# Pooled attention with a mixer behind it: the fourth batch's q right behind the third's v, two buffers for v, and the loads of two batches in a row

## The chip, the core and the metric

The kernel runs on one core of a Trainium2 chip. TensorE (PE) does the matmuls and their weight loads (PEld), VectorE (DVE), ScalarE (ACT) and GpSimd (POOL) the rest; SyncE (SP) issues transfers. All loads of inputs are issued by POOL, which casts them from float32 to bfloat16 on the way; SP issues the transposes that run as transfers, and the stores. The time is device microseconds of one execution, and a kernel's number is the median of its runs.

## What is computed

```python
B, H, S, D = 8, 8, 576, 64            # q, k, v float32
k_p = k.reshape(B, H, 72, 8, D).mean(axis=3)
v_p = v.reshape(B, H, 72, 8, D).mean(axis=3)
attn = softmax(scale * q @ k_p^T)     # 576 x 72 for each head
x = (attn @ v_p) -> (B, S, H * D)     # 8 x 576 x 512
h = relu(x^T @ w_tok1) @ w_tok2       # token mix: 576 -> 256 -> 576
u = x + h^T
out = u + relu(u @ w_ch1) @ w_ch2     # channel mix: 512 -> 1536 -> 512
```

## The kernel before

A batch has 576 rows: 512 "main" rows in four groups of 128, and 64 "tail" rows. Tails are joined in pairs of batches so that they fill 128 partitions: `groups = [[0, 7], [1, 2], [3, 4], [5, 6]]`. For the pairs [3, 4] and [5, 6] one tail unit computes the attention of both batches' tails at once. So the tail of batch 3 needs k, q and v of batch 4 as well.

For batch b the steps are: load k, q, v (`load`, L117); average k by matmuls on PE (`pool_k`, L256) into a block-diagonal operand kbd; average v. Batches 0 and 1 average v by matmuls, and from batch 2 on POOL adds the eight rows of each window (`sum_v`, L293), twelve instructions for each batch, in two-head steps, into vpx. Then come the transpose of q (from batch 2 on by SP as a transfer, `qT_dma`, L547, main and tail), scores (`do_S`, L320 and L420), row maxima and subtraction on DVE, exponentials on ACT (`do_E`), the transposes of the probabilities by SP (`do_PT`, L344 and L445, tile pT), the values (`do_AV`, L358 and L459, matmuls at L391), token mix (`do_AT` L482, `do_u` L506, transposes of u by SP at L522, tile uTm), and channel mix (`channel_mix`, L759): L773 makes GT, L788 the output.

The order on every engine is written by hand: within `manual_schedule` the emission order is the order of each engine's queue, and the loop at L853 weaves two streams for each b by their costs. The main stream is the channel mix of batch b (`c_stream`, L820); the side stream is `value_stream` of batch b + 1 (values and token mix) followed by `score_stream` of batch b + 2 (pooling of k, scores, exponentials, transposes). While c(1) runs, the side stream is thus the values of batch 2 and the scores of batch 3; within the scores of batch 3, k of batch 4 is pooled too, since it owns the shared tail (`owned`, L689).

Loads of batch 2 are issued before the loop (k and q) and early in `second_stream` (v, L659), directly ahead of `sum_v(2)`. Later loads stand behind a gate: `load_gated` (L746) lets POOL copy one column of the last pT of the current batch, so that POOL's queue goes on only when that transpose has landed; then it issues the loads of the batch and runs `sum_v`. With b = 2 the gate brings the rest of batch 3 and batch 4 (L749 to L754).

Buffers: `kv_pool` (km, qm) has two of each, `v_pool` (vs) one, `tail_pool` (kt, qt) two, `gt_pool` two for each width of GT (512 for main rows, 128 for a tail). Batch 1's tails are single tiles, and so is w2r, in which w_tok2 is staged before POOL splits it (`split_w_tok2`, L234).

Of the kernel before, what the change touches and what calls it, by code (L numbers as in the profile page):

```python
# [9 lines left out]
BF16 = mybir.dt.bfloat16  # L10
# [5 lines left out]
class Stream:  # L16
# [5 lines left out]
    def add(self, cost, fn):  # L22
        self.items.append((cost, fn))
# [25 lines left out]
def kernel(  # L49
# [18 lines left out]
    B, H, S, D = q.shape  # L68
# [14 lines left out]

    singles = ctx.enter_context(tc.tile_pool(name="singles", bufs=1))
    kv_pool = ctx.enter_context(tc.tile_pool(name="kv", bufs=2))
    v_pool = ctx.enter_context(tc.tile_pool(name="vp", bufs=1))
    sum_pool = ctx.enter_context(tc.tile_pool(name="sums", bufs=1))
    tail_pool = ctx.enter_context(tc.tile_pool(name="tl", bufs=2))
    pt_pool = ctx.enter_context(tc.tile_pool(name="ptp", bufs=6))
# [5 lines left out]
    at_pool = ctx.enter_context(tc.tile_pool(name="atp", bufs=3))  # L95
    ut_pool = ctx.enter_context(tc.tile_pool(name="utail", bufs=2))
    gt_pool = ctx.enter_context(tc.tile_pool(name="gt", bufs=2))
    out_pool = ctx.enter_context(tc.tile_pool(name="outp", bufs=4))
    ps = ctx.enter_context(tc.tile_pool(name="ps", bufs=6, space=bass.MemoryType.PSUM))
    ps_tr = ctx.enter_context(tc.tile_pool(name="ps_tr", bufs=2, space=bass.MemoryType.PSUM))  # L100
# [11 lines left out]
    tail_t[0] = tail_t[B - 1] = [singles.tile([P, H, D], BF16, name=n) for n in ("kt0", "qt0", "vt0")]  # L112
    for t in tail_t[0]:
        nc.vector.memset(t[half[1]], 0.0)
    tail_t[1] = [singles.tile([P, H, D], BF16, name=n) for n in ("kt1", "qt1", "vt1")]

    def load(b, which=(0, 1, 2)):  # L117
        g = group_of[b]
        if (b == 2 or g > 1 and slot_of[b] == 0) and 0 in which:
            tail_t[b] = [tail_pool.tile([P, H, D], BF16, name=n) for n in ("kt", "qt")]  # L120
            if b == 2:
                for t in tail_t[b]:
                    nc.gpsimd.memset(t[half[0]], 0.0)
            else:
                tail_t[groups[g][1]] = tail_t[b]
        main_t.setdefault(b, [None] * 3)
        for i in which:
            src = (k, q, v)[i]
            if i == 2 and b > 1:

                vs = v_pool.tile([P, H, POOL, D], BF16, name="vs")
                nc.gpsimd.dma_start(out=vs[0:SP].rearrange("p h t d -> p h (t d)"),
                                    in_=src[b].rearrange("h (p t) d -> p h (t d)", t=POOL))
                main_t[b][i] = vs
                continue
            mt = (v_pool.tile([P, H, POOL, D], BF16, name="vs")[:, :, 0:NJ, :] if i == 2 else
                  kv_pool.tile([P, H, NJ, D], BF16, name=("km", "qm")[i]))
            main_t[b][i], tt = mt, tail_t[b][i]
            nc.gpsimd.dma_start(out=mt.rearrange("p h j d -> p h (j d)"),
                                in_=src[b, :, 0:MAIN, :].rearrange("h (p j) d -> p h (j d)", j=NJ))  # L140

            for bb in [b] if g < 2 else groups[g] if slot_of[b] == 0 else []:
                nc.gpsimd.dma_start(out=tt[half[slot_of[bb]]], in_=src[bb, :, MAIN:S, :].rearrange("h p d -> p h d"))
# [72 lines left out]

    w1m = singles.tile([P, NJ, DT], BF16)
    w1t = [singles.tile([P, DT], BF16, name=f"w1t{s}") for s in range(2)]
    w2r = singles.tile([P, 2, S], BF16)
    w2m = singles.tile([P, 2, NJ, P], BF16)  # L220
    w2t = [singles.tile([P, 2, P], BF16, name=f"w2t{s}") for s in range(2)]
    wc1 = singles.tile([P, 4, DC], BF16)
# [426 lines left out]
    def second_stream(st):  # L649

        add = adder(st)
        b = 1
        a, c, t = units(b)
        add(KP, pool_k, b)
        add(QT, a.do_qT)
        add(QT, c.do_qT)
        add(SC, a.do_S, 0)
        add(VP, pool_v, b)
        add(0, load, 2, (2,))  # L659
        add(0, sum_v, 2)  # L660
        add(SC, a.do_S, 1)
        add(0, a.do_E, 0)
        add(SC, a.do_S, 2)
        add(0, a.do_E, 1)
        add(SC, c.do_S, 0)
        add(0, a.do_E, 2)
        add(QT, t.do_qT)
        add(SC, c.do_S, 1)
        add(0, c.do_E, 0)
        add(PT, a.do_PT, 0)  # L670
        add(SC, t.do_S)
        add(0, c.do_E, 1)
        add(PT, a.do_PT, 1)
        add(SC, c.do_S, 2)
        add(0, t.do_E)
        add(AV, a.do_AV, 0)
        add(0, c.do_E, 2)
        add(PT, t.do_PT)
        add(AV, a.do_AV, 1)
        add(PT, c.do_PT, 0)  # L680
        add(PT, c.do_PT, 1)
        add(AV, t.do_AV)
        units(2)
        add(0, qT_dma, 2)
        add(AV, c.do_AV, 0)
        add(AV, c.do_AV, 1)
        mix_stream(st, b, owned(2))
# [37 lines left out]
    def value_stream(st, b):  # L725

        add = adder(st)
        a, c, t = parts[b]
        if b == 2:
            add(0, load_gated, b + 2, lambda: c.pT[1][:, 0, 0:1])  # L730
        if b + 1 < B:
            units(b + 1)
            add(0, qT_dma, b + 1)
        if b != 2 and b + 2 < B:
            add(0, load_gated, b + 2, lambda: c.pT[1][:, 0, 0:1])
        add(AV, a.do_AV, 0)
        add(AV, a.do_AV, 1)
        if t:
            add(AV, t.do_AV)
        add(AV, c.do_AV, 0)  # L740
        add(AV, c.do_AV, 1)
        mix_stream(st, b, owned(b + 1)[:1] if b + 1 < B and b != 2 else ())

    gate = singles.tile([P, 1], BF16)

    def load_gated(b, ready):  # L746

        nc.gpsimd.tensor_copy(out=gate, in_=ready())
        if b == 4:  # L749

            load(b - 1, (1, 0, 2))
            load(b, (0, 1))
            sum_v(b - 1)
            load(b, (2,))  # L754
        else:
            load(b, (0, 2, 1) if slot_of[b] else (0, 1, 2))
        sum_v(b)

    def channel_mix(uTs, us, dst, width, early=0):  # L759

        GT = gt_pool.tile([P, NM, width], BF16, name=f"GT{width}")
        per = 512 // width

        def do_GT(m0):
            def f():
                g_ps = ps.tile([P, per, width], FP32, name="pa")
                for i in range(per):  # L770
                    m = m0 + i
                    for kk in range(4):
                        nc.tensor.matmul(out=g_ps[:, i, :], lhsT=wc1[:, kk, m * P:(m + 1) * P], rhs=uTs[:, kk, :],  # L773
                                         start=(kk == 0), stop=(kk == 3))
                nc.scalar.activation(out=GT[:, m0:m0 + per, :], in_=g_ps, func=AF.Relu)  # L775
            return f

        def out_pieces(j, halves=1):
            n, w = NM // 3, DM // halves
            pieces = []  # L780
            for c in range(halves):
                cols, hold = slice(c * w, (c + 1) * w), {}

                def do_out(part, cols=cols, hold=hold):
                    if part == 0:
                        hold["ps"] = ps.tile([P, w], FP32, name="pa")
                    for kk in range(part * n, (part + 1) * n):
                        nc.tensor.matmul(out=hold["ps"], lhsT=GT[:, kk, j * P:(j + 1) * P], rhs=wc2[:, kk, cols],  # L788
                                         start=(kk == 0), stop=(kk == NM - 1 and us is not None))
                    if part == 2:  # L790
                        o_sb = out_pool.tile([P, w], FP32, name="o")
                        if us is None:
                            for kk in range(4):
                                nc.tensor.matmul(out=hold["ps"][:, kk * P:(kk + 1) * P], lhsT=uTs[:, kk, j * P:(j + 1) * P],
                                                 rhs=ident, start=False, stop=(kk == 3))
                            nc.vector.tensor_copy(out=o_sb, in_=hold["ps"])
                        else:
                            nc.vector.tensor_tensor(out=o_sb, in0=hold["ps"], in1=us(j)[:, cols], op=ALU.add)  # L798
                        dst(j, cols, o_sb)

                for part in range(3):
                    pieces.append((864 / halves, lambda part=part, do=do_out: do(part)))
            return pieces

        def do_early(m, hold, k0):
            def f():
                if k0 == 0:
                    hold[m] = ps.tile([P, width], FP32, name="pa")
                for kk in range(k0, k0 + 2):
                    nc.tensor.matmul(out=hold[m], lhsT=wc1[:, kk, m * P:(m + 1) * P], rhs=uTs[:, kk, :],  # L810
                                     start=(kk == 0), stop=(kk == 3))
                if k0 == 2:
                    nc.scalar.activation(out=GT[:, m, :], in_=hold[m], func=AF.Relu)
            return f

        hold = {}
        wide = [(432, do_early(m, hold, k0)) for k0 in (0, 2) for m in range(early)]
        return wide + [(864, do_GT(m0)) for m0 in range(early, NM, per)], out_pieces
# [74 lines left out]
```

## Time and profile before

| | us |
|---|---|
| median of 3 runs | 305.63 |
| the runs | 301.86, 305.63, 309.34 |
| the profiled execution | 307.68 |
| its span, first to last instruction | 306.0 |
| busy PE, DVE, ACT, POOL | 280.0, 161.2, 120.7, 101.4 |
| matmuls of L788, L773 | 105.9, 94.8 |

The mean granted clock of TensorE in it is 0.961 of full. The two lines of the channel mix are the largest groups, and the chain of work that ended last runs over them, over transfers of v and over POOL's sums (columns: start, length, what):

```profile
77.18 16.25 DMA vs<-in_v_dram
...
103.66 10.29 DMA vs<-in_v_dram
114.09 1.14 POOL s L299
```

The chain's shares by engine:

```profile
PE 68%; DMA 17%; POOL 12%; issue 1%; DVE 1%; ACT 0%; POOLq 0%
```

A chain goes back from the last instruction, at each step to what released it, or to the instruction before it on its engine; PE's share is work, and the shares of DMA and POOL are stretches in which the chain ran over a transfer or over a sum. The three channel-mix stretches that matter begin, by the first L773 of a batch in PE's timeline, at 64.95 (batch 1), 107.42 (batch 2) and 153.37 (batch 3).

### The profile page before, as it was taken

Reading aid. Unit: us, or ns where it says so; the run is one execution under the profiler, and the core shown is the slowest. Engines: PE = TensorE matmul, PEld = TensorE weight load, DVE = VectorE, ACT = ScalarE, POOL = GpSimd, SP = SyncE. Lnnn points to the kernel's source line nnn. Section 1 sums busy time; section 2 is a strip of 40 time slices with the busy share of each in tenths; the row PEclk is TensorE's granted clock in tenths of the full one; section 3 lists DMA queues with packets and bytes.
Section 4 is the critical chain, followed back from the end, with each engine's and each line's share of the span. In section 5 each row is a group of like instructions: output and inputs, shape, how many; then the busy total and the mean of one; then the engine's idle time right before and its main releaser. Section 6 shows DMA issues by size and latency. Waiting matters only on the chain.

```text
span 306.0 us, 5659 instructions
## 1 busy us (share of the span) xinstructions
PE 280.0 (92%) x2242; PEld 148.3 (48%) x2242; DVE 161.2 (53%) x368; ACT 120.7 (39%) x221; POOL 101.4 (33%) x147
## 2 busy tenths in 40 slices
PE   6899999999924938799999999999999999999995
PEld 4574555555402513344654545446544444464463
DVE  4783486787522923227763795368546943430012
ACT  8573893155210423130545336405452353025420
POOL 8675500835407609908430382265000000000000
PEclk9999999999985986599999999999999999999999
DMA  7999999787999999793799999996914850152013
GB/s 89 185 204 195 200 199 161 156 155 135 178 170 125 160 146 205 81 167 106 155 193 134 145 201 220 158 173 127 216 26 86 155 138 1 71 133 56 2 69 104
DMA packets 102714, 42.68 MB, mean 139 GB/s; under 512 B 72480, under 2 KB 98080, under 8 KB 102688
## 3 DMA queue, kind: packets, MB, share of 16 engines
q0 software_dynamic: 36688, 17.93, 45.7%
q1 hardware_dynamic: 65856, 24.26, 43.5%
q8 instruction: 17, 0.28, 0.4%
q10 hardware_dynamic: 144, 0.13, 0.1%
q14 instruction: 9, 0.07, 0.1%
HBM read 35.85 MB, written 9.44 MB: 148 GB/s over the span
## 4 chain that ended last, share of the span: by engine, by line
PE 68%; DMA 17%; POOL 12%; issue 1%; DVE 1%; ACT 0%; POOLq 0%
PE pa L788 27%; PE pa L773 26%; DMA vs<-in_v_dram 13%; PE pa L510 3%; PE pa L476 3%; POOL s L299 3%; DMA w2r<-in_moe_w_tok_dram 3%; PE pa L391 2%; PE pa L327 2%; POOL s L300 2%; POOL vpx L301 1%; DMA pT<-prob_m 1%; PE pa L515 1%; PE pa L480 1%; PE pa L268 1%
## 5 line engine op out<-in xcount | busy, mean ns | idle before, releaser
L788 PE MATMUL pa<-wc,GT 128*128 128x512 bf16 (+1 forms) x444 | 105.9, 378 | 0.0
L773 PE MATMUL pa<-uTm,wc 128*128 128x512 bf16 x372 | 94.8, 395 | 0.0
L775 ACT ACTIVATE GT<-pa 128x512 bf16<-128x512 f32 x105 | 62.3, 597 | 76.3 <-PE pa L773 76.1
L773 PEld LDWEIGHTS <-wc 128*128 128x128 bf16 x564 | 46.2, 100 | 38.8 <-issue 5.1
L788 PEld LDWEIGHTS <-GT 128*128 128x128 bf16 x444 | 41.8, 99 | 40.8 <-issue 1.1
L299 POOL TENSOR_TENSOR s<-vs 72x512 f32<-72x512 bf16 x24 | 27.5, 1147 | 69.7 <-DMA vs<-in_v_dram 68.3
L340 ACT ACTIVATE prob_m<-sh 128x432 bf16<-128x432 f32 (+1 forms) x48 | 24.4, 521 | 60.9 <-DVE sh L332 51.1
L798 DVE TENSOR_TENSOR o<-pa,um 128x512 f32<-128x512 f32 (+1 forms) x29 | 19.4, 669 | 26.0 <-PE pa L788 26.0
L330 DVE TENSOR_REDUCE mx<-pa 128x6 f32<-128x432 f32 (+1 forms) x48 | 26.4, 550 | 9.4 <-PE pa L327 9.3
L395 DVE RECIPROCAL den<-pa 128x4 f32<-128x4 f32 (+1 forms) x66 | 11.7, 177 | 34.5 <-PE pa L391 34.3
L332 DVE TENSOR_TENSOR sh<-pa,mx 128x432 f32<-128x432 f32 (+1 forms) x48 | 26.8, 558 | 5.1 <-ACT GT L775 0.5
L396 DVE TENSOR_TENSOR xm<-pa,den 128x256 bf16<-128x256 f32 x56 | 23.8, 425 | 1.9
L512 DVE TENSOR_TENSOR um<-pa,xm 128x512 bf16<-128x512 f32 x28 | 18.8, 687 | 8.3 <-PE pa L510 8.3
L391 PE MATMUL pa<-vpx,pT 72*128 72x65 bf16 (+1 forms) x280 | 15.0, 199 | 7.5 <-DMA pT<-prob_m 4.7
L391 PEld LDWEIGHTS <-pT 72*128 72x128 bf16 (+1 forms) x280 | 13.2, 104 | 16.8 <-issue 5.9
L327 PE MATMUL pa<-kbd,qT 128*128 128x144 bf16 x128 | 15.9, 231 | 5.3 <-DMA qT<-qm 4.9
L327 PEld LDWEIGHTS <-qT 128*128 128x128 bf16 x128 | 10.8, 100 | 14.8 <-DMA qT<-qm 5.8
L300 POOL TENSOR_TENSOR s<-s 72x256 f32<-72x256 f32 x24 | 17.3, 722 | 1.9
L472 DVE TENSOR_SCALAR AT<-pa 128x512 bf16<-128x512 f32 x8 | 5.5, 692 | 21.7 <-PE pa L480 20.2
L510 PE MATMUL pa<-AT,w2m 128*128 128x512 bf16 x56 | 15.8, 379 | 0.0
L476 PE MATMUL pa<-xm,w1m 128*128 128x512 bf16 x56 | 14.5, 379 | 0.3 <-DVE xm L396 0.3
L254 PE MATMUL pa<-idle 128*128 128x288 bf16 (+2 forms) x36 | 9.9, 405 | 2.2 <-DVE pool_t L179 2.2
(126 smaller groups left out, 236.9 us busy)
## 6 DMA issues: line engine op xcount, KB each, us to landing
out_dram<-o SPq DMA_DIRECT2D x31, 256.0 KB, 2.6
km<-in_k_dram POOLq DMA_DIRECT2D x8, 512.0 KB, 8.9
qm<-in_q_dram POOLq DMA_DIRECT2D x7, 512.0 KB, 11.8
vs<-in_v_dram POOLq DMA_DIRECT2D x6, 576.0 KB, 12.2
wc<-in_moe_w_ch_dram POOLq DMA_DIRECT2D x6, 512.0 KB, 12.6
out_dram<-o SPq DMA_DIRECT2D x9, 128.0 KB, 2.3
vs<-in_v_dram POOLq DMA_DIRECT2D x2, 512.0 KB, 10.1
kt<-in_k_dram POOLq DMA_DIRECT2D x8, 64.0 KB, 7.8
```

The source lines that it names most:

```text
L299: nc.gpsimd.tensor_tensor(out=s4, in0=vs[:, hs, 0:4], in1=vs[:, hs, 4:8], op=add)
L327: nc.tensor.matmul(out=sc[:, (h - h0) * 2:(h - h0) * 2 + 2, :], lhsT=qTs[self.b][:, 2 * h + self.jj, :], rhs=kbd[self.b % NB][:, h], start ...
L330: nc.vector.tensor_reduce(out=mx[:, 0:n], in_=sc, axis=AX.X, op=ALU.max)
L332: nc.vector.tensor_tensor(out=sh[:, 0:n], in0=sc, in1=mx[:, 0:n, None].broadcast_to([P, n, SP]), op=ALU.subtract)
L340: nc.scalar.activation(out=self.probs[:, :, h0:h1, 0:SP].rearrange("p e h n -> p h e n"), in_=self.sh[i][:, 0:(h1 - h0) * 2].rearrange("p ...
L391: nc.tensor.matmul(out=ao[r, hh, :], lhsT=probs_of(h, r), rhs=vpx[b % NB][:, h, :], start=True, stop=True)
L396: nc.vector.tensor_tensor(out=xo[rows, hf * HP * D:(hf + 1) * HP * D].rearrange("p (h d) -> p h d", d=D), in0=ao[rows, :, 0:D], in1=den[ro ...
L476: nc.tensor.matmul(out=at_ps, lhsT=w1m[:, j, m * P:(m + 1) * P], rhs=x_main[b][:, j, :], start=(j == 0), stop=False)
L510: nc.tensor.matmul(out=u_ps, lhsT=w2m[:, m, j, :], rhs=ATs[b][:, m, :], start=(m == 0), stop=(m == 1))
L773: nc.tensor.matmul(out=g_ps[:, i, :], lhsT=wc1[:, kk, m * P:(m + 1) * P], rhs=uTs[:, kk, :], start=(kk == 0), stop=(kk == 3))
L775: nc.scalar.activation(out=GT[:, m0:m0 + per, :], in_=g_ps, func=AF.Relu)
L788: nc.tensor.matmul(out=hold["ps"], lhsT=GT[:, kk, j * P:(j + 1) * P], rhs=wc2[:, kk, cols], start=(kk == 0), stop=(kk == NM - 1 and us is ...
```

## The change

Two buffers for v; q of batch 3 (with the q tails of 3 and 4) is loaded right behind v of batch 2, ahead of `sum_v(2)` in POOL's queue; behind the gate of b = 2 the loads of batch 3 (k, v) and 4 (k, v, q) follow one another, and only then come the two `sum_v`. In `value_stream`, b = 2 now emits `units(3)` and `qT_dma(3)` ahead of the gate, as the other batches do, which leaves each engine's own order there as it was. For b = 3, 5 and 7 the tail's values go behind the two main halves. Batch 1's k and q tails come from `tail_pool`, w2r takes one of the wide GT buffers, and the narrow GT has a pool of its own with one buffer.

```diff
-    v_pool = ctx.enter_context(tc.tile_pool(name="vp", bufs=1))
+    v_pool = ctx.enter_context(tc.tile_pool(name="vp", bufs=2))
...
+    gtt_pool = ctx.enter_context(tc.tile_pool(name="gtt", bufs=1))
...
-    tail_t[1] = [singles.tile([P, H, D], BF16, name=n) for n in ("kt1", "qt1", "vt1")]
+    tail_t[1] = [tail_pool.tile([P, H, D], BF16, name=n) for n in ("kt", "qt")]
+    tail_t[1].append(singles.tile([P, H, D], BF16, name="vt1"))
 
     def load(b, which=(0, 1, 2)):
         g = group_of[b]
-        if (b == 2 or g > 1 and slot_of[b] == 0) and 0 in which:
+        if b not in tail_t:
...
-    w2r = singles.tile([P, 2, S], BF16)
+    w2r = gt_pool.tile([P, 2, S], BF16, name=f"GT{MAIN}")
...
         add(0, load, 2, (2,))
+        add(0, load, 3, (1,))
         add(0, sum_v, 2)
...
-        if b == 2:
-            add(0, load_gated, b + 2, lambda: c.pT[1][:, 0, 0:1])
         if b + 1 < B:
             units(b + 1)
             add(0, qT_dma, b + 1)
-        if b != 2 and b + 2 < B:
+        if b + 2 < B:
             add(0, load_gated, b + 2, lambda: c.pT[1][:, 0, 0:1])
         add(AV, a.do_AV, 0)
         add(AV, a.do_AV, 1)
-        if t:
+        if t and b == 2:
             add(AV, t.do_AV)
         add(AV, c.do_AV, 0)
         add(AV, c.do_AV, 1)
+        if t and b > 2:
+            add(AV, t.do_AV)
...
-            load(b - 1, (1, 0, 2))
-            load(b, (0, 1))
+            load(b - 1, (0, 2))
+            load(b, (0, 2, 1))
             sum_v(b - 1)
-            load(b, (2,))
...
-        GT = gt_pool.tile([P, NM, width], BF16, name=f"GT{width}")
+        GT = (gt_pool if width == MAIN else gtt_pool).tile([P, NM, width], BF16, name=f"GT{width}")
```

## The prediction

> **What bounds the kernel now.** I read the page's slices first, then the table of 6 us windows, then the timelines of the PE, POOL and SP queues in the stretch that the slices pick out, and last the DMA issues there. I call c(b) the channel-mix stretch of batch b (L773 then L788); c(1) runs from 64.95 to 107.42 us, c(2) to 153.37.
>
> ```profile
> PE   6899999999924938799999999999999999999995
> ...
> PEclk9999999999985986599999999999999999999999
> DMA  7999999787999999793799999996914850152013
> ```
>
> These are 40 slices of 7.65 us. After the start PE drops only in slices 12, 13 and 15 to 17 (84 to 130 us) and in the last, and the granted clock falls there. DMA is at 9 in most of the same slices. The windows (start:end, length, then PE, PEld, DVE, ACT, POOL busy, clock, DMA share, GB/s) give the sizes:
>
> ```profile
> 84.00:90.00 6.00, 1.29 (x24) 0.66 (x19) 0.69 (x2) 0.73 (x2) 0.00 (x0) 0.92 1.35 173
> 90.00:96.00 6.00, 1.14 (x4) 0.21 (x3) 0.93 (x2) 0.05 (x1) 2.27 (x3) 0.50 1.44 149
> ...
> 108.00:114.00 6.00, 1.32 (x8) 0.41 (x6) 0.95 (x2) 1.55 (x4) 0.00 (x0) 0.91 1.30 128
> 114.00:120.00 6.00, 6.00 (x29) 2.75 (x30) 2.24 (x8) 1.19 (x2) 5.44 (x7) 0.52 1.18 275
> 120.00:126.00 6.00, 3.15 (x25) 1.29 (x23) 1.21 (x4) 1.20 (x2) 5.61 (x10) 0.76 0.15 33
> ```
>
> So PE bounds the kernel everywhere except 84 to 126, and 114 to 120 is "full" only because its matmuls run at half clock. From 132 on every window but the last has PE at 6.00. PE's timeline names what ends each hole (in brackets idle before and releaser):
>
> ```profile
> 88.93 0.33 PE L272 MATMUL pa<-pool_t,kt 128*64 128x8 bf16 x8 [4.71 <-DMA kt<-in_k_dram]
> 89.19 1.89 PE L788 MATMUL pa<-wc,GT 128*128 128x512 bf16 x4
> 95.94 0.54 PE L327 MATMUL pa<-kbd,qT 128*128 128x144 bf16 x3 [4.86 <-DMA qT<-qm]
> ...
> 113.99 0.62 PE L391 MATMUL pa<-vpx,pT 72*128 72x65 bf16 x8 [4.68 <-DMA pT<-prob_m]
> 114.42 3.60 PE L773 MATMUL pa<-uTm,wc 128*128 128x512 bf16 x8
> ...
> 124.27 0.27 PE L391 MATMUL pa<-vpx,pT 72*64 72x65 bf16 x3 [2.30 <-POOL vpx L301]
> ```
>
> All four are data of batches 3 and 4. POOL and SP say why they are late:
>
> ```profile
> 72.70 0.92 POOL L139 DMA_DIRECT2D qm<-in_q_dram  x1
> ...
> 77.18 0.87 POOL L132 DMA_DIRECT2D vs<-in_v_dram  x1
> 78.02 0.93 POOL L139 DMA_DIRECT2D km<-in_k_dram  x1
> ...
> 103.66 0.86 POOL L132 DMA_DIRECT2D vs<-in_v_dram  x1
> 114.09 1.14 POOL L299 TENSOR_TENSOR s<-vs 72x512 f32<-72x512 bf16 x1 [9.57 <-DMA vs<-in_v_dram]
> ```
>
> ```profile
> 79.02 6.87 SPq L549 DMA_TRANSPOSE qT<-qm  x1
> 86.00 3.06 SPq L410 DMA_TRANSPOSE qTt<-qt  x1
> ```
>
> q3 leaves only behind the gate at 72.45, SP transposes it at 79.02 in the middle of the load burst, and that transpose lands 16.9 us later, at 95.9. v4 can't be loaded before sum_v(3) has read the single v buffer (103.66); its sums end at 124.2, and its transfer (10.3 us) lies over the transposes of batch 3's probabilities, of which the first takes 11.0 us to land against 3.5 for those issued at 113.5.
>
> **The change, part by part.**
>
> *Buffers.* w2r in a GT buffer, batch 1's tails in the tail pool, the narrow GT in one buffer: no instruction is added on any engine. w2r is last read at 19.5 us, before any GT is written (L813, from 30 on). A narrow GT is reused at the closest in c(7) after c(6), whose narrow L788 end by 276.5 and the next narrow L773 starts at 292.05. Nothing, covered by 15 us; without that cover PE would wait for a narrow block, some 3 us.
>
> *q3 early.* Three POOL issues (0.9 and 2 x 0.68 us) move from 72.7 to about 37.7, ahead of sum_v(2). The small ones wait for batch 1's tail transposes on PE (38.38) and, by the lanes, for the third piece of wc2 (issued 29.01, median 12.6 us to landing: 41.6). sum_v(2) behind them waits for v2 until 53.84 anyhow: 12 us of cover. v2 itself is ahead of q3 in queue 0. What does stand beside it is the transpose of q2: issued 45.70, landed 9.6 us later at 55.3, when queue 0 was empty. From 45 to 50 us queue 0 moved 0.86 MB (2056 packets) and SP's queue 0.04 MB (145 packets): loads starve transposes. q3's 0.64 MB at 0.172 MB/us add 3.7 us, so qT(2) lands at 59.0, and S(2) on PE stands at 57.97: 1.0 us late, carried through c(1). Bounds: 0 (SP gets the idle share) and 3.7; I take 1.0.
>
> [...]
>
> *qT(3) at once.* SP is idle from 71.2 to 79.02; the transpose now goes at about 71.2, and queue 0's burst moves its first bytes at about 74.2 (the slices of that window are near 0 before). Free transposes of this kind land in 3.8 us (issued 117.36), so by about 76, and S(3) needs it at 86. The 4.86 us wait goes; its cover is those 10 us.
>
> *k3 first.* km3 takes q3's place, which landed 6.3 us after its issue: 79.0. kt follows with 0.13 MB. PE needs it at 84.2. The 4.71 us go too; at worst kt takes its old 11.5 us from issue, 86, and 1.8 us stay.
>
> *The new next wait.* In c(1) PE then comes to k4's pooling 3.0 us after L272 ends, at 87.2 (L788 x4 0.86, kbd copies 0.93, S, L788 x4, S). Queue 0 must have sent kt, v3 and k4 behind km3, 1.22 MB. Its rate beside transposes: 93.5 to 102.2 two loads of 0.51 MB (k4 landed 97.6, q4 102.2), 0.118 MB/us; the burst from 83.5 (k3 landed) to 102.2, 1.73 MB, 0.093; both queues together, 4.1 MB from 74.2 to 102, 0.15. With 0.118, the row whose transposes are those of u, as now: 79.0 + 10.3 = 89.3, or 90.3 with the 1.0 us shift of gate and all behind it. PE waits 90.3 - 88.2 = 2.1 us. Ends: 0 at 0.15, 4 to 5 at 0.093.
>
> *Sum for c(1).* The halved clock costs L788 1.89 for 1.03 and 1.91 for 1.03, S .54 and .57 for .35, pooling 1.00 for .69: 2.5 us, gone. From k4's pooling to the end were 8.94 us, 8.6 at full clock. c(2) starts at 90.3 + 8.6 = 98.9, instead of 107.42.
>
> [...]
>
> *v4 and c(2).* v3 lands at 80.0 + 0.70/0.118 = 86.0, its sums take 10.1 (93.57 to 103.7): 96.1. v4 lands at 95.2, before that; its sums end at 106.3. The tail's AV is moved behind the two others: on PE it stands some 9.5 us into c(2), 108.4. No wait, 2 us of cover; if v4 is 4 us later, 2 us stay. SP can take the first pair of pT(3) 3.9 us after k4's pooling (the third exponential, 101.96 + 0.44 against 98.48), at 94.2, beside the last 5 us of q4 (landing at 99.5); c(2) wants it at 100.8. The others find no load in flight: 3.5 us to landing. Gone are 4.68 + 0.55 + 2.30 = 7.5 us of waits and the half clock of 114 to 130: L773 3.60, 2.62, 3.60, 2.71 for 1.89 each, 5.0, and AV 0.6. c(2) was 45.95 and becomes 32.8; c(4), of the same kind, is 32.4. I add 0.5 for a late first pT (0 to 3). c(2) ends at 98.9 + 32.8 + 0.5 = 132.2.
>
> *Later batches.* From 153.37 PE is full in every window, so the rest stays 152.6. Tail's AV behind the main ones at batches 5 and 7: AT's fifth matmul needs it, 0.86 us after its mains start, while two reciprocals and products take 1.2: 0 to 0.4 each, taken as 0. Load(5)'s gate opens 18 us sooner, at about 106: same place in c(2) as for later batches.
>
> *Total.* 306.0 - (153.37 - 132.2) = 284.8 us of span; the profiled execution took 307.68, 1.68 more than its span: 286.5. That execution was 2 us above the median of 305.63, out of runs from 301.86 to 309.34; the waits that go are what made it long, so I take off half a microsecond: **286**.
>
> **Rivals.** All hang on queue 0's rate r beside transposes, so they can be told apart.
>
> *Half delivered.* r near 0.093 and q3 costing its 3.7: k4 lands at 79.0 + 3.7 + 13.1 = 95.8, PE waits about 5 us with the clock halved (2.5), c(2) starts at 106.9 at the latest; c(2)'s 13.1 go, though pT late by 3 gives some back: 294 to 299. For it: two loads in a row were that slow. Against: they shared with a 0.5 MB transpose that is now out of the way.
>
> *Moves but does not shrink.* r = 0.070 (kt and v3, 0.70 MB, took from 83.5 to 93.5): k4 lands at 96.4 or later, q4 at 112, and pT(3) again falls into a load. Then c(1) ends near 108, pT takes its 11 us, c(2) is long: 300 to 308, no change.
>
> *Slower.* The same burst with v4 in it starves everything: below r = 0.055, k4 comes at 101 or later, c(2) starts at 112, pT(3) waits till q4 has landed at 120 or later, and PE stands with half the clock through c(2): 312 to 320. It decides from r under about 0.055, a fifth below the lowest rate seen, which is what speaks against it.
>
> **Chances.** Forecast (281 to 291) 0.62, half delivered 0.24, no change 0.09, slower 0.05. Two per cent of 305.63, 6 us, is about what a measurement tells from none: under 299.5 counts as faster, so 0.86, 0.09, 0.05. The low end: no shift and r = 0.15 put k4 at 87, c(2) at 95.8 and the total at 283, and the runs' spread (1.2% either way) puts a median near 279.5. The high end goes into the half-delivered case, to 297, which leaves about 0.2 outside.
>
> **What would show it.** PE's timeline after: no wait for kt or qT(3); a wait of 0 to 4 us at the second pooling of k in c(1), by km; AV(3) without a wait over 1 us; c(2) starting near 99 and about 33 long. SP: qT(3) near 72, landing within 6. POOL: two sets of v sums with no DMA issue between, the second ending near 106. Granted clock above 0.98 (0.961 before). Wrong would be: S(2) over 3 us late (q3 costs more than said), km4 landing after 93, or pT(3) landing 8 us or more after issue.

## The result and the profile after

The changed kernel takes 290.84 us (median of 4, 289.09 to 291.64) against 305.69 (median of 4, 301.86 to 309.34) beside it: a ratio of 0.9546, 95% interval 0.9445 to 0.9648. A second set of runs (`e11_after_again`) gave 289.51 and 0.9565 (0.9495 to 0.9636). The ratios leave out executions more than 1.5% above the fastest of their kernel, so they are not the quotients of the medians, and the profiled execution of before is itself one of those long ones. It took 307.68 with a span of 306.0; that of the changed kernel took 290.76 with a span of 289.0. The line numbers of the changed kernel are 2 to 3 higher (L773 is now L775, L788 is L790, L391 is L393, L327 is L329, L522 is L524).

The page's slices, for the same three rows:

```profile
PE   6799999979993999999999999999999999999995
...
PEclk9999999999998699999999999999999999999999
DMA  7999999998999999988999799959523930241013
```

One hole is left (slice 13, around 90 us) and a small new one (slice 9, 58 to 65). The windows of 6 us over the old holes, in the same columns:

```profile
84.00:90.00 6.00, 4.28 (x60) 2.28 (x58) 4.64 (x9) 1.35 (x3) 2.62 (x4) 1.00 1.39 175
90.00:96.00 6.00, 2.65 (x45) 1.86 (x47) 1.14 (x3) 1.35 (x3) 5.49 (x7) 0.64 1.42 150
...
108.00:114.00 6.00, 5.95 (x54) 2.96 (x53) 3.36 (x12) 3.62 (x7) 4.10 (x7) 1.00 1.03 200
114.00:120.00 6.00, 5.95 (x42) 2.86 (x40) 1.81 (x5) 2.36 (x4) 1.46 (x2) 1.00 1.60 174
120.00:126.00 6.00, 6.00 (x31) 2.73 (x29) 3.86 (x6) 0.00 (x0) 0.00 (x0) 1.00 1.13 172
```

From 96 on PE is full, after 98.5 also at full clock; the windows from 108 to 126, which had 1.32, a half-clock 6.00 and 3.15, are now full at full clock. PE's timeline names the two waits that remain:

```profile
59.80 0.36 PE L329 MATMUL pa<-kbd,qT 128*128 128x144 bf16 x3 [1.86 <-DMA qT<-qm]
...
66.78 3.62 PE L775 MATMUL pa<-uTm,wc 128*128 128x512 bf16 x16
...
88.09 0.35 PE L329 MATMUL pa<-kbd,qT 128*128 128x144 bf16 x3
93.02 1.06 PE L270 MATMUL pa<-pool_m,km 128*64 128x64 bf16 x32 [4.58 <-DMA km<-in_k_dram]
...
96.10 1.91 PE L790 MATMUL pa<-wc,GT 128*128 128x512 bf16 x4
...
104.08 1.89 PE L775 MATMUL pa<-uTm,wc 128*128 128x512 bf16 x8
105.81 0.42 PE L393 MATMUL pa<-vpx,pT 72*128 72x65 bf16 x8
...
113.86 0.45 PE L393 MATMUL pa<-vpx,pT 72*64 72x65 bf16 x16
```

The first is the scores of batch 2, which wait for q2's transpose; the second the pooling of k4, with the clock at half behind it (1.06 for 0.69, 1.91 for 1.03). No wait for kt, qT(3), pT or vpx of batches 3 and 4 is left. POOL's and SP's timelines:

```profile
73.82 0.92 POOL L141 DMA_DIRECT2D km<-in_k_dram  x1
...
76.08 0.85 POOL L134 DMA_DIRECT2D vs<-in_v_dram  x1
76.92 0.91 POOL L141 DMA_DIRECT2D km<-in_k_dram  x1
77.81 0.84 POOL L134 DMA_DIRECT2D vs<-in_v_dram  x1
...
87.14 1.14 POOL L301 TENSOR_TENSOR s<-vs 72x512 f32<-72x512 bf16 x1 [7.59 <-DMA vs<-in_v_dram]
...
107.10 0.45 POOL L303 TENSOR_TENSOR vpx<-s 72x128 bf16<-72x128 f32 x1
```

```profile
72.42 1.83 SPq L551 DMA_TRANSPOSE qT<-qm  x1
74.35 1.23 SPq L412 DMA_TRANSPOSE qTt<-qt  x1
```

q3's transpose goes at 72.42 and lands 3.8 us later, instead of 79.02 and 16.9. v3's sums begin at 87.1 (93.6 before), v4's follow without a load between and end at 107.6 (124.2 before). By stretches:

| | before | after |
|---|---|---|
| c(1) begins | 64.95 | 66.78 |
| c(1) long | 42.47 | 37.30 |
| c(2) long | 45.95 | 32.42 |
| from c(3) to the end | 152.6 | 152.5 |

So +1.8, -5.2, -13.5 and -0.1 make the 17.0 us between the two spans. The medians differ by 14.9, so these stretches overstate the gain by some 2 us. The trace's clock records have PE at half clock for 23.9 us in all before (stretches of 10.24, 6.83 and 6.83, without the last us of the run), and for 6.83 after.

### The profile page after: what moved, and what is told of

Same layout as the page of the kernel before. It is cut to its first block, busy times and chain, and to the rows that moved or that the text cites. A ratio compares the mean times of both kernels' runs of the same rounds, so it can differ in the third digit from the quotient of the medians.

```text
span 289.0 us, 5626 instructions
## 1 busy us (share of the span) xinstructions
PE 270.8 (94%) x2206; PEld 146.2 (51%) x2242; DVE 161.2 (56%) x368; ACT 120.9 (42%) x221; POOL 101.8 (35%) x147
## 4 chain that ended last, share of the span: by engine, by line
PE 73%; DMA 19%; POOL 5%; issue 1%; ACT 0%; DVE 0%; POOLq 0%
PE pa L790 30%; PE pa L775 28%; DMA km<-in_k_dram 6%; DMA qT<-qm 5%; DMA vs<-in_v_dram 4%; DMA GT<-in_moe_w_tok_dram 3%; PE pa L512 3%; PE pa L478 3%; PE pa L329 2%; PE pa L393 2%; DMA pT<-prob_m 1%; PE pa L270 1%; PE pa L517 1%; PE pa L482 1%; POOL kt L145 1%
## 5 line engine op out<-in xcount | busy, mean ns | idle before, releaser
L790 PE MATMUL pa<-wc,GT 128*128 128x512 bf16 (+1 forms) x428 | 104.0, 378 | 1.3 <-issue 0.6
L775 PE MATMUL pa<-uTm,wc 128*128 128x512 bf16 x357 | 88.7, 379 | 0.7
L775 PEld LDWEIGHTS <-wc 128*128 128x128 bf16 x564 | 45.0, 98 | 35.8 <-issue 0.2
L790 PEld LDWEIGHTS <-GT 128*128 128x128 bf16 x444 | 41.8, 99 | 40.9 <-issue 1.3
L329 PE MATMUL pa<-kbd,qT 128*128 128x144 bf16 x128 | 15.8, 228 | 2.3 <-DMA qT<-qm 1.9
L393 PEld LDWEIGHTS <-pT 72*128 72x128 bf16 (+1 forms) x280 | 12.5, 100 | 8.2 <-issue 1.7
L329 PEld LDWEIGHTS <-qT 128*128 128x128 bf16 x128 | 10.7, 99 | 11.5 <-DMA qT<-qm 2.4
L393 PE MATMUL pa<-vpx,pT 72*128 72x65 bf16 (+1 forms) x280 | 13.9, 194 | 0.1
L775 PE MATMUL pa<-uTt,wc 128*128 128x128 bf16 x192 | 11.9, 219 | 0.0
```

The costliest lines, as they stand in the source:

```text
L329: nc.tensor.matmul(out=sc[:, (h - h0) * 2:(h - h0) * 2 + 2, :], lhsT=qTs[self.b][:, 2 * h + self.jj, :], rhs=kbd[self.b % NB][:, h], start ...
L393: nc.tensor.matmul(out=ao[r, hh, :], lhsT=probs_of(h, r), rhs=vpx[b % NB][:, h, :], start=True, stop=True)
```

## The experiments

Theory: the early q3 takes the waits out of c(1), the early v4 those out of c(2), and k4's landing is the next late thing. Rivals: one of the three edits (q3, second v buffer, tail moved) does it all; or k4's wait only stands for a burst of loads that ends no sooner. Each run's ratio is to the kernel of before on the same chip, whose medians were 302.6 to 304.8; the brackets are 95% intervals, which is 1 to 3 us each way.

**The second buffer without the early q3** (`e1_v_only`).

```diff
-        add(0, load, 3, (1,))
...
+        if b == 2:
+            add(0, load_gated, b + 2, lambda: c.pT[1][:, 0, 0:1])
         if b + 1 < B:
...
-            load(b - 1, (0, 2))
+            load(b - 1, (1, 0, 2))
             load(b, (0, 2, 1))
```

> The changed kernel with q3 put back: q of batch 3 is loaded behind the gate again, ahead of its k (and the gate stands ahead of the SP transpose, as before the change); two buffers for v, the six loads in a row and the tail order stay. Theory (the early q3 removes the first stretch of waits, the early v4 the second, separately): c(1) is as long as before or some us longer, since qT(3) is again transposed inside a burst that now holds v4 too: wait for qT(3) of 5 to 9 us, c(2) starting at 107 to 111. c(2) keeps its 32 to 34, so 294 to 299 us. Rival (c(2) became short because everything ahead of it came early or because the tail's values moved, not by v4): c(2) stays above 40 and the time is 303 or more.

297.36 us, 0.9839 (0.9781 to 0.9897). PE's timeline:

```profile
88.86 0.38 PE L274 MATMUL pa<-pool_t,kt 128*64 128x8 bf16 x8 [3.43 <-DMA kt<-in_k_dram]
97.96 0.54 PE L329 MATMUL pa<-kbd,qT 128*128 128x144 bf16 x3 [6.91 <-DMA qT<-qm]
...
113.30 0.43 PE L393 MATMUL pa<-vpx,pT 72*128 72x65 bf16 x8 [1.59 <-DMA pT<-prob_m]
```

The two old waits of c(1) are back, qT's longer, and c(2) begins at 109.82; it is 34.2 long all the same, and the time is in the theory's range. The tail's values stay moved in this run, so it does not tell the second buffer from the tail.

**The early q3 without the second buffer** (`e2_q_only`).

```diff
-    v_pool = ctx.enter_context(tc.tile_pool(name="vp", bufs=2))
+    v_pool = ctx.enter_context(tc.tile_pool(name="vp", bufs=1))
...
-            load(b, (0, 2, 1))
+            load(b, (0, 1))
             sum_v(b - 1)
+            load(b, (2,))
```

> The changed kernel with one buffer for v, and v4 loaded behind sum_v(3) as before the change; q3 early, the tail order and the room stay. Theory: c(1) is as in the changed kernel (wait for k4 4 to 5 us, c(2) starting near 104), since v4 stands behind k4 in the burst anyhow. v4 is issued near 97 and lies over the transposes of batch 3's probabilities (pT landing 8 to 11 us after issue instead of 3.5) and its sums end near 118, so c(2) gets waits of 5 to 9 us and half the clock for a while: 40 to 46 long, 297 to 304 us. Rival (the early q3 does it all, the buffer is idle): within 1.5 us of the 290.8 of the changed kernel.

293.68 us, 0.9784 (0.9674 to 0.9893): between before and after, 3.3 us under the theory's range and above the rival's. c(2) is 36.2 long. PE's timeline:

```profile
90.89 1.06 PE L270 MATMUL pa<-pool_m,km 128*64 128x64 bf16 x32 [2.66 <-DMA km<-in_k_dram]
106.22 0.43 PE L393 MATMUL pa<-vpx,pT 72*128 72x65 bf16 x8 [2.00 <-DMA pT<-prob_m]
```

v4 does lie over pT (2.00 us of wait, and half clock again), but there is no wait for vpx. Two things made it cheaper than expected. With q3 out of the burst, v3 lands at 86.5 and not 93.4, so that even the one buffer comes free at 96.7 (103.66 before). And k4's wait is 1.9 us shorter, with v4 out of the burst behind it (2.93 in `e5_q_tail_first`, which has the same loads). That leaves the moved tail as what hides v4's sums, which end near 116.

**The moved tail, with two buffers and with one** (`e3_tail_first`, `e5_q_tail_first`): the same edit, on the changed kernel and on `e2_q_only`.

```diff
-        if t and b == 2:
+        if t:
             add(AV, t.do_AV)
...
-        if t and b > 2:
-            add(AV, t.do_AV)
```

> The changed kernel with the tail's values of batches 3, 5 and 7 back between the two main halves. Theory: worth nothing, because sum_v(4) ends at 107.6 and the tail's matmuls would stand at about 110: within 1 us of 290.8, no wait for vpx. Rival (the move is what takes away the wait for vpx of batch 4): a wait of 1 to 4 us for vpx in c(2), 292 to 296 us.

> The run with one buffer for v and q3 early (293.7 us), with the tail's values of batches 3, 5 and 7 put back between the main halves as before the change. Theory: the move of the tail is what hid the late v4 there: sums of v4 end near 116, the tail stood at about 116 and now stands at about 111, so PE waits some 5 us for vpx in c(2), the clock falls, 297 to 302 us. That would make the early q3 and the moved tail together, not the second buffer, the larger part of what c(2) gained. Rival (c(2) was short there only because v4 came earlier, and the tail's place is worth nothing, as with two buffers): 293 to 295 us.

With two buffers 290.27 us (0.9654, 0.9628 to 0.9681), the same as the changed kernel, and no wait for vpx. With one buffer 299.34 (0.9944, 0.9906 to 0.9982). PE's timeline of the latter:

```profile
112.20 0.25 PE L393 MATMUL pa<-vpx,pT 72*64 72x65 bf16 x4 [2.28 <-POOL vpx L303]
114.75 0.30 PE L393 MATMUL pa<-vpx,pT 72*64 72x65 bf16 x4 [2.30 <-POOL vpx L303]
117.30 0.27 PE L393 MATMUL pa<-vpx,pT 72*64 72x65 bf16 x3 [2.25 <-POOL vpx L303]
```

The tail's matmuls now follow POOL's sums head pair by head pair, the clock is at half for 6.8 us from 114.8 on, and c(2) is 44.5 long. So the second buffer and the moved tail cover the same wait, for vpx of batch 4: the tail's place is worth 5.7 us by the medians without the buffer (two chips) and nothing with it, and with the tail moved the buffer is worth another 3 to 4. And the early q3 alone brings about half a per cent by its ratio: c(1) is 34.6 long, but c(2) waits and is nearly as long as before. Without the early q3, the buffer and the tail were not parted.

**The clock behind k4's wait** (`e4_warm`).

```diff
+        if b == 3:
+            add(0, warm, 16)
         for bb in own[1:]:
             add(KP, pool_k, bb)
```

> The changed kernel with 16 matmuls of zeros (512 columns, 3.5 us at full clock) on PE ahead of the pooling of k4, inside the 4.6 us in which PE waits for it; it computes nothing that is used. Theory: the wait for k4 halves the clock, and that costs 2.5 to 3 us from 93 to 100: with the filler the pooling takes 0.7 instead of 1.06, the L788 groups behind it 1.03 instead of 1.9, c(2) starts near 101.4 and the time is 287.5 to 288.5. Rival (after the wait PE is bound by something else that is late as well, scores or SP, so a full clock finds other waits): 290 to 291.5, with idle time in place of slow matmuls.

289.37 us, 0.9642 (0.9579 to 0.9706): 1.5 us under the changed kernel's first set, level with its second. PE's timeline:

```profile
92.22 0.69 PE L270 MATMUL pa<-pool_m,km 128*64 128x64 bf16 x32 [0.48 <-DMA km<-in_k_dram]
103.48 0.43 PE L393 MATMUL pa<-vpx,pT 72*128 72x65 bf16 x8 [0.74 <-DMA pT<-prob_m]
```

The half clock is gone (the pooling takes 0.69) and c(2) begins at 100.85, 3.2 us sooner, as expected. But pT then waits, and c(3) begins only 2.3 us sooner. The median lies between the two ranges: theory and rival are both partly right.

**k4's wait taken away, in two ways** (`e6_pool_late`, `e7_k4_first`). In the first, PE comes to k4 later; in the second, k4 comes sooner.

```diff
+        late = b == 3
+        if not late:
+            for bb in own[1:]:
+                add(KP, pool_k, bb)
...
+        if late:
+            add(KP, pool_k, 4)
+            add(2 * SC, t.do_S)
+            add(0, t.do_E)
+            add(0, t.do_PT)
```

```diff
-            load(b - 1, (0, 2))
-            load(b, (0, 2, 1))
+            load(b - 1, (0,))
+            load(b, (0,))
+            load(b - 1, (2,))
+            load(b, (2, 1))
```

> The changed kernel with the pooling of k4 and the tail's scores of batches 3 and 4 behind all main scores of batch 3, not between them. Theory: k4 lands at 93 and PE comes to it at about 95 instead of 88.4, so the wait of 4.6 us and the half clock behind it (some 3 us) go; c(2) starts near 97 to 98. What is late next is the first transposes of batch 3's probabilities, beside the last load (q4 landing near 100), 1 to 3 us. 284.5 to 288 us. Rival (queue 0 is the bound, and whatever PE does first only changes the name of the wait: uT of batch 2 and pT of batch 3 land no sooner than 100 to 103): 289 to 291.5 us.

> The changed kernel with k4 loaded ahead of v3 in the burst (k3, k4, v3, v4, q4). Theory: k4 lands near 87, the wait of 4.6 us in c(1) goes and c(2) starts near 97 to 98; but v3 lands near 93 instead of 87, its sums end at 103, and the first values of c(2), due at 99 to 100, wait 3 to 5 us for vpx: most of it is given back, 287 to 291 us. Rival (POOL's sums have slack): no wait for vpx and 283 to 285 us.

289.57 us (0.9611, 0.9549 to 0.9673) and 288.51 (0.9591, 0.9543 to 0.9638). In PE's timeline, first of `e6_pool_late`, then of `e7_k4_first`:

```profile
92.32 0.69 PE L270 MATMUL pa<-pool_m,km 128*64 128x64 bf16 x32 [0.19 <-DMA km<-in_k_dram]
...
103.47 0.43 PE L393 MATMUL pa<-vpx,pT 72*128 72x65 bf16 x8 [3.00 <-DMA pT<-prob_m]
```

```profile
99.61 1.89 PE L777 MATMUL pa<-uTm,wc 128*128 128x512 bf16 x8 [2.25 <-DMA uTm<-um]
103.27 0.43 PE L393 MATMUL pa<-vpx,pT 72*128 72x65 bf16 x8 [1.77 <-DMA pT<-prob_m]
```

k4's wait is gone in both, and c(2) begins at 98.6 and 99.6 instead of 104.1, 5.5 and 4.5 us sooner; of that, 0.7 and 2.0 are left at the start of c(3). The last transposes of u of batch 2 and the first of batch 3's probabilities land only when the burst is over. In `e7_k4_first` those of u take 10 to 13.5 us to land and the first of the probabilities 9.9, those issued from 102.87 on 3.1 to 3.3. The first range was missed: 289.57 is the rival's. The second was hit, but the wait for vpx that I expected there did not come; the transposes were later still. To see whether its 2.3 us are real, both kernels ran again on one chip (`e11_after_again`, `e12_k4_first_again`).

> The changed kernel as it is, beside the one with k4 first, on one chip. Theory: 289 to 292 us, the wait for k4 of 4 to 5 us and half the clock behind it in the profile. Rival (the 290.8 was that chip's): outside of that by more than 2 us.

> The kernel with k4 ahead of v3, beside the changed one on the same chip. Theory (c(2) can begin sooner but then waits for transposes, so about half of the 4.6 us wait and the half clock is kept as gain): 1.5 to 3 us under the changed kernel, 287.5 to 289.5 us. Rival (the difference of 2.3 us lay between the chips): within 1 us of it.

289.51 (288.34 to 291.31) and 289.49 (289.13 to 290.36): no difference, as the rival of the second had it. The 2.3 us lay between the sets of runs, not between the kernels. k4's wait in the changed kernel is 4.33 this time, with 6.83 us of half clock again.

**The burst made shorter** (`e9_k4_first_q4_late`, `e10_q4_late`): q4 leaves the burst and is issued behind the sums of v3, with k4 first and in the changed kernel's own order. The edit shown is that of the second; the first makes the same move in the order of `e7_k4_first`.

```diff
-            load(b, (0, 2, 1))
+            load(b, (0, 2))
             sum_v(b - 1)
+            load(b, (1,))
```

> The run with k4 ahead of v3 (288.5 us), with q4 moved out of the burst: it is issued behind the sums of v3, at about 102, ahead of those of v4. Theory (what is left in c(1) and at the start of c(2) is that SP's transposes land only when queue 0 has run dry): the burst ends 4 us sooner, near 96, so uT of batch 2 lands before c(2) wants it (wait of 2.25 gone) and the first pT of batch 3 lands within 5 us (wait of 1.8 gone); c(2) starts near 97.5; q4 then lies beside the last pT, which cost 0 to 2. 285 to 287.5 us. Rival (those transposes are slow for another reason, their own packets on SP's queue): the waits stay, 288 to 290 us.

> The changed kernel (k3, v3, k4, v4 in its own order) with q4 issued behind the sums of v3, at about 97. Theory: q4 was behind everything that PE waited for there, so k4 still lands at 92 to 93 and the wait of 4.6 with its half clock stays; q4 now lies beside the first pT of batch 3, which wait 1 to 4 us: 290 to 294 us. Rival (each load in flight slows the others, so that k4 comes earlier without q4): wait for k4 under 3 us, 287 to 289 us.

290.51 us (0.9626, 0.9556 to 0.9696) and 291.77 (0.9665, 0.9587 to 0.9743). In PE's timeline of `e9_k4_first_q4_late`:

```profile
100.25 0.37 PE L393 MATMUL pa<-vpx,pT 72*128 72x65 bf16 x6 [1.57 <-DMA pT<-prob_m]
101.50 0.22 PE L393 MATMUL pa<-vpx,pT 72*128 72x65 bf16 x2 [0.88 <-POOL vpx L303]
```

The wait for u is gone, as the theory had it, c(2) begins at 96.8, and the first pT lands in 7.5 us instead of 9.9. So part of the transposes' delay is the loads beside them. But now the sums of v3 are the last (v3 comes behind k4), another 1.1 us of waits, most of it for the sums of v4, stand later, the clock falls for 3.4 us, and c(3) begins at 135.1, no sooner. The range of 285 to 287.5 was missed. `e10_q4_late` came out in its theory's range, with a wait of 2.07 for pT. But k4's wait did not stay: it is 3.27 instead of 4.58, so k4 does come sooner with less behind it, as the rival said, if less than the rival said.

**q3 somewhere else** (`e8_q_behind_sums`).

```diff
-        add(0, load, 3, (1,))
         add(0, sum_v, 2)
+        add(0, load, 3, (1,))
```

> The changed kernel with q3 issued behind the sums of v2 (POOL free at about 64) instead of ahead of them. Theory: q3's load beside the transpose of q2 is what costs the 1.9 us wait ahead of the scores of batch 2; it goes, c(1) starts at about 65, but the load now lies beside the transposes of batch 2's probabilities (64 to 71), which land some 2 to 4 us later, and the gate opens later: 289.5 to 293 us. Rival (nothing is in the way there, SP's transposes find DMA time enough): 288 to 289 us.

295.03 us, 0.9807 (0.9761 to 0.9852), worse than expected. In SP's and PE's timelines:

```profile
64.43 6.12 SPq L349 DMA_TRANSPOSE pT<-prob_m  x2
```

```profile
67.80 5.30 PE L775 MATMUL pa<-uTm,wc 128*128 128x512 bf16 x16 [2.31 <-DVE sh L334]
```

The wait ahead of the scores of batch 2 is gone, but c(1) begins at 67.80, not at 65, behind a wait of 2.31 (the subtraction named is an early one; what PE reads there is uTm, whose last transposes took 4.0 us to land, beside q3), with the clock at half for 3.4 us; batch 2's first probabilities take 8.6 us to land instead of 3.2, and the gate opens at 77.3 instead of 73.6. Right behind v2, q3 costs 1.9 us; 25 us later it costs more than twice that.

## Why the prediction held, step by step

The forecast case came true (286 predicted, 290.84 measured), in a stretch-by-stretch sum that was too low in three terms of c(1) and nearly exact elsewhere. The three were off the same way, so the result lies only 0.16 us inside the range's upper end of 291; that it is inside at all is partly luck, since the runs spread over 2.5 us. Some signs that the prediction set itself were missed or just met: the wait at the second pooling of k is 4.58 and not 0 to 4, c(2) starts at 104.1 and not near 99, and k4 lands at 92.97 where landing after 93 would have counted as wrong. In c(1) what came is in kind the case "half delivered", a wait of nearly 5 us with the clock halved behind it; k4's landing at 93.0 lies halfway between the forecast's 90.3 and that case's 95.8.

*q3 early* was mis-sized: 1.0 us predicted for the wait at batch 2's scores, 1.86 measured (0.4 to 2.6 in the other profiles with q3 there). q2's transpose landed 14.3 us after its issue, at 59.8. The cause is the one named, q3's load beside that transpose; the 3.7 us added were 4.5, and the wait lasts until that landing. But "loads starve transposes", 145 packets to 2056, took in a stretch in which the transposes had no packet moving yet: before, from 47.5 to 50, it was 145 packets to 825, 1 to 6, and in the changed kernel it was none for 4 us and then 1280 to 1319, 1 to 1 (last section). The small loads did wait "by the lanes" as said: the second left at 43.05 after 1.63 us for a piece of wc, and the sums of v2 behind it still waited 10.20 us for v2.

*qT(3) at once* held: issued at 72.42, landed in 3.8. *k3 first* held: k3 landed after 7.4 us (6.3 predicted), kt without a wait.

*The new next wait* was the right one and mis-sized: 2.1 us predicted, 4.58 measured. PE came at 88.4 (88.2 predicted); k4 landed at 93.0 (90.3). Of these 2.7 us, 1.25 are k3, which landed at 81.25 and not at 80.0. The rest is the rate: queue 0 sent kt, v3 and k4, 1.22 MB, from 81.25 to 93.0, 0.103 MB/us, where I had taken 0.118 out of 0.093 to 0.15. The row was chosen for its transposes, but its stretch had the end of the burst in it, and what stands behind k4 was given no part in the sum. The runs show that it has one: without v4 in the burst k4's wait is 2.66 and 2.93 (`e2_q_only`, `e5_q_tail_first`), without q4 3.27 (`e10_q4_late`), with both 4.3 to 5.1.

*Sum for c(1)*: from k4's pooling to the end 8.6 us were predicted at full clock, 11.06 measured, because the wait of 4.58 halved the clock (filled in `e4_warm`, it left the pooling at 0.69 and not 1.06). That a wait of 2.1 leaves the clock full was my estimate, and no run shows it to hold in general: the clock was at half behind a wait of 2.07 in `e10_q4_late` (the values behind it took 0.56 for 0.42) and from 1.2 us into one of 2.30 in the kernel before, while one of 2.25 in `e7_k4_first` left it full. k4's landing (2.7) and the clock (2.5) are the 5.2 us by which c(2) began late, 104.08 for 98.9. The profile shows half clock from 91.67 to 98.50, 6.83 us of which 1.35 were still wait, and a loss of 2.5. The prediction's "half clock of 114 to 130" in the kernel before was a misreading: the clock records have half clock from 112.92 to 119.75, full clock, and half again from 123.16 to 129.99, behind the wait of 2.30 for vpx.

*v4 and c(2)*: 33.3 predicted, 32.42 measured, sums of v4 ending at 107.6 (106.3), tail at 113.9, 9.8 into c(2) (9.5). The total was right, but the step put it down to the second buffer, with the tail's move as cover. `e2_q_only` and `e5_q_tail_first` show that the early q3 and the moved tail already give 9.7 of the 13.5 us (c(2) 36.2 long with the one buffer), since v3, and with it the single buffer, comes 7 us sooner. That v4 was held back by q3 at the head of the burst was in the profile of before, and I read it only as v3's late landing.

*Later batches*: 152.6 predicted, 152.5 measured; no tail cost seen at batches 5 and 7.

Of the rivals, "moves but does not shrink" was wrong as a forecast of the whole and nearer the truth one step further: from the changed kernel on, no edit of the order took more than 2.4 us off its first median or 1.0 off its second, and the one that ran again beside it showed no gain. With k4's wait, with a transpose's or with POOL's in its place, c(3) begins between 134.2 and 136.5 in `after`, `e4_warm`, `e6_pool_late`, `e7_k4_first` and `e9_k4_first_q4_late`, while c(2)'s start moves over 7 us. In `e10_q4_late`, which waits for both k4 and pT, it is 138.4. There was little left to win: from c(1) to c(3) PE's own work at full clock is 62 to 64 us in every profile, and the rest, its idle time (the filler of `e4_warm` included) and what the half clock adds, is 25.6 us before, 7.6 in `after`, and 4.5 to 6.9 in the other four. That this rest is held by the data of batches 3 and 4 together (five loads, the transposes beside them and 20 us of sums) is my reading; which of these would give way first to a change of size, and not of order, was not tried.

## What to carry to other kernels

When a wait is taken away, look at what is landing just behind it in the same burst: here four orders of the same loads moved the last waits from k to transposes to sums, and the medians stayed between 288.5 and 291.8 us. Two edits that cover the same wait (a second buffer, a later consumer) must be tried one by one and together, since here one alone shows most of the gain and the other all of it. And a transfer that is moved early is paid for where it lands, here q3 with 1.86 us at the scores of batch 2. Ask which transposes run beside it there.

## What the runs showed of the hardware

In three bursts here a transpose that SP issued behind POOL's casting loads moved its first packet only 3.8 to 4.2 us after its issue; from there on its queue moved about as many packets as theirs. q2's transpose in the changed kernel is issued at 45.50. Queues 0 (loads) and 1 (transposes and stores), packets, MB and share of the engines' time, from 45.5 to 49.5 us and from 49.5 to 56:

```profile
q0 software_dynamic: 1805, 0.77, 147.2%
```

```profile
q0 software_dynamic: 1319, 0.71, 86.2%
q1 hardware_dynamic: 1280, 0.33, 55.1%
```

In the first stretch queue 1 moves nothing; in the second it moves 1280 packets to queue 0's 1319. The transposes of u do the same in the next burst: the first is issued at 81.33, its first packet moves at 85.16, and from 85 to 93 queue 1 moves 1555 packets to 1650. In the kernel before, q3's transpose of 79.02 moves its first packet at 83.25, and from there to 95.9 it is 2563 packets to 2354; only q2's of 45.70, with fewer loads behind it, moves its first after 2.0 us. Equal counts are dear for a transpose all the same: queue 1's packets are of some 250 bytes in that second stretch (0.33 MB in 1280) and the loads' of some 550 (0.71 in 1319), and where no load was in flight (before, 54 to 55 us) queue 1 moved 1151 packets in 1 us, beside the loads 1280 in 6.5.

Nor are the counts equal everywhere: from 47.5 to 50 us before, queue 1 had 145 packets to 825. What holds the first packet back for 4 us no run here shows; in those three cases 0.76 to 0.77 MB of loads go ahead of it.

The half clock lasted, the end of each run apart, 10.24, 6.83 and 6.83 us in the kernel before and 6.83 in the changed one; by the clock of the windows it was about 13.6 us in `e1_v_only`, 6.8 and 3.5 in `e2_q_only`, and 3.4 in `e10_q4_late`, all of them close to whole multiples of 3.41, the third part of 10.24. The length of a wait does not decide it alone: 2.66 us halved the clock before the wait was over in `e2_q_only` (at 90.27, 2.04 us into it, pooling 1.06), 5.07 did so for only some 3.4 us in `e3_tail_first`, behind 3.27 us in `e10_q4_late` the pooling still ran at 0.69, the half clock coming after it, and 2.25 us in `e7_k4_first` did not halve it at all. What sets the moment at which the clock falls, no run here shows.
